# Linear attention on one Trainium2 core: the gate's product turned round and taken four steps at a time, and the lower weight halves subtracted from copies in PSUM

## The chip, the cores and the metric

The kernel runs on one core of a Trainium2 chip. The metric is device time in microseconds (us) of one execution; three runs gave 673.35, 677.05 and 677.16, median 677.05. TensorE is PE in the rows (its weight loads are PEld), VectorE is DVE, ScalarE is ACT, GpSimd is POOL, and SP issues most DMAs.

## What is computed

Three stages in a row, all on 3072 tokens of width 384 (4 sequences of 768 tokens, 8 heads of 48).

```python
for t in range(S):                       # stage 1: linear attention with decay
    cur = einsum('bhd,bhe->bhde', u * kt, vt)
    y[:, :, t] = einsum('bhd,bhde->bhe', rt, state + cur)
    state = w[None, :, :, None] * state + einsum('bhd,bhe->bhde', kt, vt)
logits = x @ w_gate                      # stage 2: 8 experts of exactly 384 tokens each,
h = maximum(x[mask] @ w1[e], 0.0)        #   given out greedily by descending logit
out[mask] = h @ w2[e]
h = maximum(maximum(x @ w1, x @ w2), x @ w3)   # stage 3
return h @ w_out
```

## The kernel before

**Attention** (class `Attention`) goes through 24 steps i, each 128 tokens of one sequence: `steps` is (b, c) for c in 0..5, b in 0..3, so four steps in a row share a chunk number c. Per step and line:

- GpSimd (POOL) does five multiplications of SBUF tiles: `decayed` (L129, `rt`), `natural` (L184, `kp`), `bonus` (L192, L193, `rk`) and, in `extra`, L203 (`bv`).
- TensorE makes transposes of keys (`turn`, L213, `pT`), masked scores (`scores`, L227, `pA`), output rows from the state and from the scores (`rows`, L248, both into `pY`), the new state (`state`, L281, `pK`), a transpose of the output (`cross`, L302, `pX`), four matmuls on ones whose result is not used (`keep`, L237), and the gate's logits (`gate`, L313). In `gate`, the step's transposed output `xt` (128x128 for each of three pieces) is the stationary operand and the 128x8 gate weights move.
- VectorE (DVE) masks the scores (L230, `am`), sums the bonus (L201, `bon`), adds the output parts (L263, `x`) and the state (L285, `st`). ScalarE (ACT) copies `kt` (L215), scales the state (L293, `S`), copies `xt` (L304) and takes squares of the output (L305).

Each engine works through its list in program order and waits by semaphores. `run` writes that order out step by step: step i issues `load(i + 4)`, `across(i + 3)` (the DMA of `rt`), `store(i - 1)`, then the POOL work for steps ahead, `turn(i + 2)`, `fade(i - 1)`, `scores(i + 1)`, `extra(i + 1)`, `cross(i - 1)`, `keep`, `rows(i)`, `gate(i - 2)`, `state(i)`.

**Weights.** Between these, at four places per step (`side`), a `Feed` issues pieces of the work that readies the first weights of the later stages: each fp32 (or float64) weight is scaled and split into an upper fp16 half, which ACT writes (L695 for `w`, L801 for `v`), and a lower half, which DVE writes as raw*scale - upper in one SCALAR_TENSOR_TENSOR (L699, L804); both its tensor inputs lie in SBUF. The float64 weights are first made fp32 with integer instructions on DVE (L760, L767, L776) that also read SBUF alone. Each piece has a cost by which the feed is spread over the steps. The early weights are `w1[0]`, `w2[0]`, the first two of stage 3, and the upper halves of `w1[1]`.

PSUM has eight banks: pX, pT, pK, lg one each, pA and pY two each. `lg` holds the logits of all steps (192 columns) and, in its upper half, the target of `keep`.

After attention come the **routing**, a chain of short dependent instructions, and the **experts** with stage 3, which are matmuls on TensorE almost throughout; the change leaves both alone but for the first input of routing, `raw` (L364), copied from `lg`.

The start is a chain too: POOL fills constants (L68 to L135), DVE waits for the first of its tables (L1173, `part`) before it builds the decay tables, and POOL's first `kp` waits for those.

Of the kernel before, what the change touches and what calls it, by code (L numbers as in the profile page):

```python
# [44 lines left out]
class Attention:  # L45


    def __init__(self, ctx, tc, K, r, rt, k, v, w, u, wg, x_dram, spare, routing):
# [10 lines left out]
        self.LD, self.RN, self.KN, self.BV, self.RT, self.KT, self.AM, self.X, self.XT, self.RK = ({} for _ in range(10))  # L59
# [17 lines left out]
        for t in self.S:  # L77
            nc.gpsimd.memset(t[:, :, D:], 0.0)
        self.routing.fill()
# [6 lines left out]
        self.wg = self.tabs.tile([128, 3, E], F32, name="wg")  # L86
        nc.sync.dma_start(self.wg, ap(wg, 0, [[E, 128], [128 * E, 3], [1, E]]))
# [4 lines left out]
        for i in range(2):  # L92
# [4 lines left out]
        self.lg = self.bank[:, :NT * E].rearrange("p (m e) -> p m e", e=E)  # L97
        nc.tensor.matmul(self.bank[:, 256:], self.K.onesf.bitcast(BF16)[:, :128], self.K.onesf.bitcast(BF16), start=True, stop=True,
                         skip_group_check=True)
# [94 lines left out]

    def extra(self, i):
# [3 lines left out]
        vn = self.LD[i][2]  # L199
        s = work.tile([128, H], F32, name="bon")  # L200
        nc.vector.tensor_reduce(s, self.RK[i].rearrange("p (h d) -> p h d", h=H), AX.X, OP.add)  # L201
# [31 lines left out]
    def keep(self, n):  # L233

        ones = self.K.onesf.bitcast(BF16)
        for _ in range(n):
            self.nc.tensor.matmul(self.bank[:, 256:], ones[:, :128], ones, start=False, stop=True, skip_group_check=True)  # L237

    def rows(self, i):
# [31 lines left out]
    def state(self, i):  # L271
# [5 lines left out]
        pk = psum.tile([128, NP, WIDE], F32, name="pK")  # L277
        for j in range(NP):
            for s in range(2):
                h = 2 * j + s  # L280
                nc.tensor.matmul(pk[64 * s:64 * s + 64, j, :], kd[:, h, :], vn[:, h * D:h * D + WIDE],  # L281
                                 start=j == 0, stop=j == NP - 1, skip_group_check=True)
        if c:
            t = work.tile([128, NP, D], F32, name="st", bufs=1)
# [11 lines left out]
    def cross(self, i):  # L296
# [6 lines left out]
        xt = self.XT[i] = work.tile([128, 3, C], F32, name="xt", bufs=3)  # L303
# [1250 lines left out]
```

## Time and profile before

| | |
|---|---|
| runs (median of 3) | 677.05 us (673.35 to 677.16) |
| profiled execution | 679.12 us, of which 677.4 us from the first to the last instruction |
| busy share of the span | PE 95%, PEld 63%, DVE 58%, ACT 52%, POOL 35% |
| attention | from the start to about 159 us |
| routing | about 159 to 204 us |
| experts and stage 3 | about 204 us to the end, PE 462.19 us busy of 473.40 |
| mean granted TensorE clock | 0.957 of full speed |

Busy time counts instructions that run, side by side or not; the end of a matmul is modelled, so a busy PE is not PE at its peak. The numbers below are of the one profiled execution, which is 2.07 us above the median of the runs.

### The profile page before, as it was taken

The page shows a single profiled execution, that of the slowest core. Times are in us where ns is not written, and L with a number is a line of the kernel's source. Part 1 is how long each engine was busy: PE and PEld are TensorE (multiplying, and loading weights), DVE is VectorE, ACT ScalarE, POOL GpSimd, SP SyncE. Part 2 cuts the span into 40 slices and gives each one's busy share as a digit, 9 for nine tenths or more (in the row PEclk, how much of TensorE's full clock was granted, in tenths as well). Part 3 has the DMA queues.
Part 4 walks back from the last instruction along what each step waited for, and adds up shares of the span by engine and source line. Part 5 has one row for each costly group of instructions (what it writes and reads, how often), then busy time and mean ns, then how long its engine had stood idle before and what let it go on. Part 6 is the DMA issues. An engine that isn't in the chain of part 4 may idle for free.

```text
span 677.4 us, 14362 instructions
## 1 busy us (share of the span) xinstructions
PE 642.2 (95%) x5660; PEld 429.9 (63%) x5660; DVE 394.8 (58%) x1027; ACT 350.2 (52%) x782; POOL 238.2 (35%) x268
## 2 busy tenths in 40 slices
PE   6999899998779998999999999999999999999996
PEld 4788787887566664666666666656665666666663
DVE  7777988757745767774556366354626544451321
ACT  3567474854443557574755655546544545332321
POOL 6989999980150003231122023112202111110222
PEclk8889998996579999999999999999999999999999
DMA  8877876625054309064134135112414200000000
GB/s 223 291 233 226 292 223 183 210 81 210 2 156 82 142 3 204 28 125 144 59 117 118 47 129 117 48 59 71 117 47 129 53 30 13 24 1 1 36 1 35
DMA packets 54763, 72.98 MB, mean 108 GB/s; under 512 B 21408, under 2 KB 42016, under 8 KB 54688
## 3 DMA queue, kind: packets, MB, share of 16 engines
q1 hardware_dynamic: 51616, 62.55, 31.3%
q0 software_dynamic: 3072, 9.44, 4.8%
q8 instruction: 46, 0.75, 0.5%
q14 instruction: 29, 0.24, 0.1%
HBM read 58.41 MB, written 9.44 MB: 100 GB/s over the span
## 4 chain that ended last, share of the span: by engine, by line
PE 60%; issue 7%; DVE 2%; POOL 1%; ACT 1%; POOLq 0%; DVEq 0%
PE pg L932 29%; PE ps L932 23%; PE px L1027 8%; POOL gt L1014 1%; DVE top L1009 1%; ACT gt L1013 0%; POOL out_dram L1034 0%; PE px L914 0%; POOLq L1550 0%; DVE da L760 0%; ACT top L1007 0%; ACT x2s L989 0%; ACT junk L628 0%; DVE sc L435 0%; DVE xr L905 0%
## 5 line engine op out<-in xcount | busy, mean ns | idle before, releaser
L932 PE MATMUL pg<-x2s,v 128*128 128x384 f16 x1296 | 217.0, 326 | 2.7 <-ACT top L1007 2.7
L932 PEld LDWEIGHTS <-v 128*128 128x128 f16 x1296 | 126.8, 98 | 86.8 <-issue 3.2
L1014 POOL TENSOR_TENSOR gt<-top,gt 128x384 f16<-128x384 f32 x48 | 44.4, 925 | 341.3 <-ACT gt L1013 291.9
L932 PEld LDWEIGHTS <-w 128*128 128x128 f16 x1242 | 117.2, 99 | 73.1 <-issue 1.6
L1009 DVE SCALAR_TENSOR_TENSOR top<-pg,sc,top 128x384 f32<-128x384 f32 x96 | 59.1, 616 | 75.0 <-PE pg L932 66.2
L932 PE MATMUL ps<-ht,w 128*128 128x384 f16 x576 | 94.9, 326 | 0.0
L699 DVE SCALAR_TENSOR_TENSOR w<-stage,sc,w 128x512 f16<-128x512 f32 (+1 forms) x80 | 70.4, 903 | 41.1 <-ACT w L695 40.8
L932 PE MATMUL ps<-xt,w 128*128 128x384 f16 (+1 forms) x540 | 88.6, 317 | 0.2 <-issue 0.2
L1013 ACT ACTIVATE gt<-top 128x384 f16<-128x384 f32 x48 | 25.0, 522 | 111.6 <-DVE top L1009 109.4
L1027 PE MATMUL px<-wo,gt 128*128 128x384 f16 x432 | 72.2, 326 | 1.8 <-POOL spacer L1033 1.0
L695 ACT ACTIVATE w<-stage,sc 128x512 f16<-128x512 f32 (+1 forms) x80 | 62.0, 797 | 3.0 <-DVE sc L466 1.2
L1027 PEld LDWEIGHTS <-gt 128*128 128x128 f16 x432 | 41.9, 98 | 30.8 <-POOL spacer L1033 1.7
L628 ACT ACTIVATE junk<-stage 128x768 bf16<-128x768 f32 x64 | 53.6, 837 | 6.3 <-DMA stage<-in_moe_w_dram 5.6
L962 DVE SCALAR_TENSOR_TENSOR ht<-ps,ht 128x384 f16<-128x384 f32 x56 | 30.9, 555 | 32.0 <-ACT ht L961 31.9
L1034 POOL DMA_INDIRECT out_dram<-o,ids x24 | 23.8, 993 | 40.8 <-ACT o L1032 40.8
L973 ACT ACTIVATE x<-ps 128x384 f32<-128x384 f32 x24 | 11.8, 490 | 49.7 <-PE ps L932 49.7
L230 DVE TENSOR_TENSOR am<-pA,mask 128x512 f32<-128x512 f32 x48 | 30.8, 682 | 10.3 <-PE pA L227 10.2
L1007 ACT ACTIVATE top<-pg,sc 128x384 f32<-128x384 f32 x48 | 27.7, 576 | 17.6 <-PE pg L932 17.2
L961 ACT ACTIVATE ht<-ps 128x384 f16<-128x384 f32 x56 | 26.7, 481 | 16.1 <-PE ps L932 16.0
L129 POOL TENSOR_TENSOR rt<-rt,tr 128x512 f32<-128x512 f32 x22 | 31.6, 1438 | 1.3 <-DMA rt<-in_rt_dram 1.3
L227 PE MATMUL pA<-rt,kt 64*128 64x128 f32 x384 | 29.9, 295 | 2.0 <-DVE am L230 1.9
L184 POOL TENSOR_TENSOR kp<-kn,tkn 128x384 f32<-128x384 f32 (+1 forms) x25 | 28.3, 1135 | 4.4 <-ACT tkn L168 3.8
(238 smaller groups left out, 851.9 us busy)
## 6 DMA issues: line engine op xcount, KB each, us to landing
stage<-in_moe_w_dram SPq DMA_DIRECT2D x41, 768.0 KB, 5.2
kn<-in_k_dram SPq DMA_DIRECT2D x24, 192.0 KB, 5.0
rn<-in_r_dram SPq DMA_DIRECT2D x24, 192.0 KB, 5.4
v<-in_v_dram SPq DMA_DIRECT2D x24, 192.0 KB, 3.2
rt<-in_rt_dram SPq DMA_DIRECT2D x48, 96.0 KB, 3.5
x_rows<-x SPq DMA_DIRECT2D x24, 192.0 KB, 2.6
stage<-in_moe_w_out_dram SPq DMA_DIRECT2D x3, 768.0 KB, 6.3
xg<-x_rows,ids POOLq DMA_INDIRECT x24, 5.1
```

Of the source, the lines that this page charges most:

```text
L129: (engine or self.nc.gpsimd).tensor_mul(self.RT[i], self.RT[i], self.tr)
L184: self.nc.gpsimd.tensor_mul(self.KN[i][:, heads, :D], kn[:, heads], self.tkn[:, heads, :D])
L227: nc.tensor.matmul(pa[s][:, j, :], kt[FULL[s], j * C:(j + 1) * C], rt[FULL[s], j * C:(j + 1) * C], start=True, stop=True, skip_group_check ...
L230: nc.vector.tensor_mul(am[:, s], pa[s], self.mask[:, None, :].to_broadcast([128, NP, C]))
L628: self.nc.scalar.activation(self.K.junk, x, AF.Square, accum_out=total)
L695: nc.scalar.activation(hi, raw, AF.Copy, scale=st["s"])
L699: nc.vector.scalar_tensor_tensor(lo, raw, st["s"], hi, op0=OP.mult, op1=OP.subtract)
L932: nc.tensor.matmul(p[:, rows], w[:, wi, k, cols], x[:, xi, k, rows], start=k == 0 and wi + xi == 0, stop=k == kb - 1 and xi == 1, skip_gro ...
L962: nc.vector.scalar_tensor_tensor(h[:, 1, f], p, 0.0, h[:, 0, f], op0=OP.max, op1=OP.subtract)
L1009: nc.vector.scalar_tensor_tensor(t, p, self.ratio[i], top, op0=OP.mult, op1=OP.max)
L1014: nc.gpsimd.tensor_sub(gt[:, 1, g], top, gt[:, 0, g])
L1027: nc.tensor.matmul(p, gt[:, gi, g, a * 128:(a + 1) * 128], self.WO[:, wi, g, :], start=g == 0 and gi + wi == 0, stop=g == self.KG - 1 and ...
```

## The change

Four edits inside attention and the feed.

1. `gate` makes the padded gate weights (128x32 per piece) the stationary operand and lets `xt` move; the three pieces write three groups of 32 partitions of `part`, and the four steps of a chunk lie in 8 rows each of those. It runs every fourth step, for four steps at once (in the last chunk step by step). ACT copies `part` to SBUF, and one step later a matmul with `sums` adds the three groups and turns the result (`logits`); ACT copies it to `raw`. So the single copy of `raw` at the end becomes six small ones. `xt` gets six buffers.
2. `keep` goes; `rows` instead issues four matmuls on zeros into `pY`, between the state's part and the scores' part, from the second chunk on. The gate stands between the two as well.
3. For the early weights, ACT copies each upper half from SBUF into one PSUM bank, `lane` (`twin`), and DVE's subtraction reads that copy. The pieces become 512 wide (some were 768), with a lower cost each.
4. `state` writes into the upper half of the `lg` bank, which frees the bank for `lane`; in the first chunk DVE now copies the state out. Also: the bonus sum is issued earlier (`summed`), the DMA of `rt` moves from the start of a step to its end (`across(i + 4)`, in place of `across(i + 3)`), and POOL fills two more constants at the start (`wg`, `zeros`).

```diff
+        self.wg = self.tabs.tile([128, 3, 56], F32, name="wg")
+        nc.gpsimd.memset(self.wg, 0.0)
+        nc.gpsimd.memset(self.zeros, 0.0)
         self.routing.fill()
...
+        nc.sync.dma_start(self.wg[:, :, 24:32], ap(wg, 0, [[E, 128], [128 * E, 3], [1, E]]))
...
+        between()
+        for n in range(KEEP if c else 0):
+            nc.tensor.matmul(py[n % 2].rearrange("p j n -> p (j n)"), self.zeros[:, :128], self.zeros, start=False, stop=False,
+                             skip_group_check=True)
         for j, s, u in where:
             h = 2 * j + s
...
-        pk = psum.tile([128, NP, WIDE], F32, name="pK")
+        pk = self.pk
...
         else:
-            t = pk
-        self.ST[i] = t
+            nc.vector.tensor_copy(t, pk[:, :, :D])
...
     def gate(self, i):
+
         if i < 0:
             return
-        b, c = self.steps[i]
-        m = b * NC + c
-        for j in range(3):
-            self.nc.tensor.matmul(self.lg[:, m, :], self.XT[i][:, j, :], self.wg[:, j, :],
-                                  start=(i == 0 and j == 0), stop=j == 2, skip_group_check=True)
+        c, k = divmod(i, B)
+        for n in (range(B) if k == B - 1 else ()) if c < NC - 1 else (k,):
+            for j in range(3):
+                self.nc.tensor.matmul(self.part[32 * j:32 * j + 32], self.wg[:, j, 24 - E * n:56 - E * n],
+                                      self.XT[B * c + n][:, j, :], start=n == 0, stop=n == B - 1, skip_group_check=True)
+        if k == B - 1:
+            self.parts = self.work.tile([128, 128], F32, name="parts", bufs=1)
+            self.nc.scalar.activation(self.parts[:96], self.part[:96], AF.Copy)
+
+    def logits(self, i):
+        c, k = divmod(i, B)
+        if k or c < 1:
+            return
+        nc, K = self.nc, self.K
+        nc.tensor.matmul(self.lg, self.parts[:96], K.sums[:96], start=True, stop=True, skip_group_check=True)
+        nc.scalar.activation(K.raw.rearrange("p (b c) e -> p b c e", c=NC)[:, :, c - 1, :],
+                             self.lg.rearrange("p (b e) -> p b e", e=E), AF.Copy, scale=-1.0)
...
+    def twin(self, x):
+
+        t = self.lane[:, :x.shape[-1]]
+        self.nc.scalar.activation(t, x, AF.Copy)
+        return t
...
         def lower(n):
             raw, (hi, lo) = part(*parts[n])
+            if apart:
+                hi = self.twin(hi)
             nc.vector.scalar_tensor_tensor(lo, raw, st["s"], hi, op0=OP.mult, op1=OP.subtract)
 
         def split(n):
             def go():
+                if n and apart:
+                    lower(n - 1)
                 if n < len(parts):
                     upper(n)
...
+            def go():
+                if j:
+                    hi, lo = (whole(dst[:, t])[:, cut(j - 1)] for t in range(2))
+                    nc.vector.scalar_tensor_tensor(lo, whole(st["x"])[:, cut(j - 1)], st["s"], self.twin(hi), op0=OP.mult,
+                                                   op1=OP.subtract)
+                if j < pieces:
+                    nc.scalar.activation(whole(dst[:, 0])[:, cut(j)], whole(st["x"])[:, cut(j)], AF.Copy, scale=st["s"])
```

TensorE, before, a step of the second chunk from the rows' state part on (`pY<-S`) to the first matmul of `keep` in the next step:

```order
L248 MATMUL pY<-S_117,rt_107 64x64 x16
L248 MATMUL pY<-v_120,am 64x64 x16
L313 MATMUL lg<-wg,xt 128x8 x3
L281 MATMUL pK<-v_120,kp_113 64x64 x8
L213 MATMUL pT<-identf,kp_112 128x128 x4
L227 MATMUL pA<-rt_109,kt_111 128x128 x8
L302 MATMUL pX<-identf,x 128x128 x3
L237 LDWEIGHTS onesf
L237 MATMUL lg<-onesf 128x256
```

TensorE, now, the same step, which is one with the gate for four steps (twelve matmuls); four pairs on zeros follow it, of which the first stands here:

```order
L307 MATMUL pX<-identf,x 128x128 x3
L250 MATMUL pY<-S_120,rt_110 64x64 x16
L319 MATMUL lg<-xt,wg 32x128 x12
L260 LDWEIGHTS zeros
L260 MATMUL pY<-zeros 128x256
```

The gate's three matmuls per step went from behind the rows' second part to twelve between its parts, and the four idle matmuls from in front of the first part to behind it.

TensorE, now, what comes next in that step, with its waits (names in brackets are the engines and DMA queues waited for):

```order
L250 MATMUL pY<-v_123,am 64x64 [waits DMAHW1_49]
L250 MATMUL pY<-v_123,am 64x64 x15
L287 MATMUL lg<-v_123,kp_116 64x64 [waits Activation_49]
L287 MATMUL lg<-v_123,kp_116 64x64 x7
L221 MATMUL pT<-identf,kp_115 128x128 [waits PE_49,Pool_49]
```

The state's matmul (L287, target now in the `lg` bank) waits for ScalarE here, that is for the copy of `part` out of the same bank.

ScalarE, before, while the first weight is split (`w_637`, pieces of 512):

```order
L305 ACTIVATE junk,norms<-x 128x384
L695 ACTIVATE w_637<-stage,sc_630 128x512 x3
L215 ACTIVATE kt_110<-pT 128x512
L293 ACTIVATE S_119<-pK,w_305 128x48 x4
L695 ACTIVATE w_637<-stage,sc_630 128x512 x2
L304 ACTIVATE xt<-pX 128x384
```

ScalarE, now, at the same place (`lane` is the copy in PSUM):

```order
L310 ACTIVATE junk,norms<-x 128x384
L649 ACTIVATE lane<-w_633 128x512
L726 ACTIVATE w_633<-stage,sc_626 128x512
L649 ACTIVATE lane<-w_633 128x512
L726 ACTIVATE w_633<-stage,sc_626 128x512
L649 ACTIVATE lane<-w_633 128x512
L726 ACTIVATE w_633<-stage,sc_626 128x512
L223 ACTIVATE kt_113<-pT 128x512
L298 ACTIVATE S_122<-st,w_310 128x48 x4
L649 ACTIVATE lane<-w_633 128x512
L726 ACTIVATE w_633<-stage,sc_626 128x512
```

Between two ScalarE instructions of attention's own chain, `xt` and `kt`, there are now six of the feed instead of three.

## Rows read from the trace of the kernel before

**Rows 1.** Windows: us; PE, PEld, DVE, ACT, POOL busy (count); clock; DMA share, GB/s.
```profile
41.00:151.00 110.00, 106.15 (x2046) 91.17 (x2046) 89.92 (x168) 71.08 (x188) 105.51 (x89) 0.98 0.66 206
```

**Rows 2.** Timeline of PE, one step: start us, us, line, out<-in, count.
```profile
130.77 0.69 PE L248 MATMUL pY<-S,rt 64*64 64x64 f32 x32
131.40 1.15 PE L248 MATMUL pY<-v,am 128*64 128x64 f32 x32
132.48 0.83 PE L313 MATMUL lg<-wg,xt 128*128 128x8 f32 x6
133.24 0.69 PE L281 MATMUL pK<-v,kp 128*64 128x64 f32 x16
...
135.92 0.60 PE L237 MATMUL lg<-onesf 128*128 128x256 bf16 x4
136.45 0.29 PE L248 MATMUL pY<-S,rt 64*64 64x64 f32 x4
```

**Rows 3.** Groups of POOL by form, 41 to 137 us: count | busy us, mean ns.
```profile
L129 POOL TENSOR_TENSOR rt<-rt,tr 128x512 f32<-128x512 f32 x16 | 24.0, 1500 | 1.3 <-DMA rt<-in_rt_dram 1.3
L193 POOL TENSOR_TENSOR rk<-rk,ub 128x384 f32<-128x384 f32 x15 | 19.1, 1272 | 1.2
L184 POOL TENSOR_TENSOR kp<-kn,tkn 128x384 f32<-128x384 f32 x15 | 18.3, 1223 | 0.6 <-PE pK L281 0.6
...
L203 POOL TENSOR_TENSOR bv<-v,bon 128x384 f32<-128x384 f32 x15 | 17.0, 1136 | 0.9 <-DVE bon L201 0.9
```

**Rows 4.** The same groups, 137 to 152 us.
```profile
L129 POOL TENSOR_TENSOR rt<-rt,tr 128x512 f32<-128x512 f32 x3 | 3.8, 1278 | 0.0
...
L193 POOL TENSOR_TENSOR rk<-rk,ub 128x384 f32<-128x384 f32 x3 | 3.0, 995 | 0.2
L203 POOL TENSOR_TENSOR bv<-v,bon 128x384 f32<-128x384 f32 x3 | 2.5, 827 | 0.0
L184 POOL TENSOR_TENSOR kp<-kn,tkn 128x384 f32<-128x384 f32 x2 | 2.0, 994 | 0.0
```

**Rows 5.** Timeline of POOL, a stretched multiplication.
```profile
65.92 1.98 POOL L129 TENSOR_TENSOR rt<-rt,tr 128x512 f32<-128x512 f32 x1
```

**Rows 6.** Timeline of DVE at the same time.
```profile
65.46 3.26 DVE L699 SCALAR_TENSOR_TENSOR w<-stage,sc,w 128x768 f16<-128x768 f32 x2
```

**Rows 7.** Groups of DVE by form, 41 to 151 us.
```profile
L230 DVE TENSOR_TENSOR am<-pA,mask 128x512 f32<-128x512 f32 x36 | 23.1, 682 | 5.4 <-PE pA L227 5.3
...
L767 DVE SCALAR_TENSOR_TENSOR da<-stage,da 128x768 int32<-128x768 int32 x6 | 9.2, 1537 | 0.1
L804 DVE SCALAR_TENSOR_TENSOR v<-wo,sc,v 128x768 f16<-128x768 f32 x6 | 8.3, 1417 | 0.0
L776 DVE SCALAR_TENSOR_TENSOR wo<-stage,da 128x768 int32<-128x768 int32 x6 | 8.2, 1372 | 0.0
L699 DVE SCALAR_TENSOR_TENSOR w<-stage,sc,w 128x512 f16<-128x512 f32 x6 | 5.8, 1000 | 0.0
L699 DVE SCALAR_TENSOR_TENSOR w<-stage,sc,w 128x768 f16<-128x768 f32 x4 | 5.6, 1425 | 0.0
```

**Rows 8.** Groups of ACT by form, 41 to 151 us.
```profile
L215 ACT ACTIVATE kt<-pT 128x512 f32<-128x512 f32 x18 | 10.7, 593 | 17.9 <-PE pT L213 17.8
...
L695 ACT ACTIVATE w<-stage,sc 128x512 f16<-128x512 f32 x8 | 5.4, 719 | 0.0
...
L628 ACT ACTIVATE junk<-wo 128x768 bf16<-128x768 f32 x6 | 5.1, 843 | 17.9 <-DVE wo L776 17.9
```

**Rows 9.** Windows around a drop of the clock (columns as in rows 1).
```profile
32.60:39.40 6.80, 6.80 (x57) 5.50 (x59) 2.70 (x10) 4.47 (x14) 6.02 (x7) 0.50 0.63 189
```

**Rows 10.** Timeline of DVE at the start.
```profile
3.58 0.15 DVE L1196 TENSOR_SCALAR pe_i<-part 128x1 int32<-128x1 int32 x1 [2.24 <-POOL part L1173]
```

**Rows 11.** Timeline of POOL at the start: constants.
```profile
1.66 1.44 POOL L76 MEMSET rt<- 128x512 f32 x3
```

**Rows 12.** Timeline of ACT at the end of attention.
```profile
158.68 0.33 ACT L364 ACTIVATE raw<-lg 128x192 f32<-128x192 f32 x1 [0.42 <-PE lg L313]
```

More of the change, by code (lines that the diff above doesn't have):

```diff
@@ L58, in __init__ @@
         self.steps = [(b, c) for c in range(NC) for b in range(B)]
-        self.LD, self.RN, self.KN, self.BV, self.RT, self.KT, self.AM, self.X, self.XT, self.RK = ({} for _ in range(10))
+        self.LD, self.RN, self.KN, self.BV, self.RT, self.KT, self.AM, self.X, self.XT, self.RK, self.BON = ({} for _ in range(11))
+        self.lane = self.psum.tile([128, 512], F32, name="lane")
+        self.zeros = self.tabs.tile([128, 256], BF16, name="zeros")
+        K.sums = self.tabs.tile([128, 32], F32, name="sums")
         wcol = self.tabs.tile([128, NP], F32, name="wcol")
@@ L96, in __init__ @@
         self.bank = self.psum.tile([128, 512], F32, name="lg")
-        self.lg = self.bank[:, :NT * E].rearrange("p (m e) -> p m e", e=E)
-        nc.tensor.matmul(self.bank[:, 256:], self.K.onesf.bitcast(BF16)[:, :128], self.K.onesf.bitcast(BF16), start=True, stop=True,
-                         skip_group_check=True)
+        self.lg, self.part = self.bank[:, :32], self.bank[:, 32:160]
+        self.pk = self.bank[:, 256:].rearrange("p (j n) -> p j n", n=WIDE)
     def clear(self, t):
@@ L231, in scores, with rows @@
         self.AM[i] = am
[L233 to L239, printed above, removed]
+    def rows(self, i, between=lambda: None):
         nc, psum = self.nc, self.psum
@@ L318, in run @@
         self.load(3)
+        self.across(3)
         feed.ahead(2)
@@ L345, in run @@
             side(3)
+            self.logits(i - 2)
             if i < NT - 2:
                 self.cross(i - 1)
-                self.keep(KEEP)
-                self.rows(i)
+                self.rows(i, lambda: self.gate(i - 2))
             else:
@@ L355, in run @@
                 self.cross(i - 1)
-            self.gate(i - 2)
+                self.gate(i - 2)
+            self.across(i + 4)
             side(4)
@@ L362, in run @@
         self.gate(NT - 1)
-        K = self.K
-        nc.scalar.activation(K.raw, self.lg, AF.Copy, scale=-1.0)
+        self.logits(NT)
 class Consts:
@@ L686, in part @@
                 return blocks[j].get()[:, q * 512:q * 512 + 512], [st["w"][:, t, q, j * 512:j * 512 + 512] for t in range(2)]
+            if apart:
+                n = (3 * j + q) * 512
+                return blocks[j].get()[:, q * 512:q * 512 + 512], [
+                    st["w"][:, t].rearrange("p k n -> p (k n)")[:, n:n + 512] for t in range(2)]
             k = 4 * j + 2 * q
@@ L689, in part @@
                 st["w"][:, t, k:k + 2].rearrange("p k n -> p (k n)") for t in range(2)]
-        parts = [(j, q) for j in range(2) for q in range(3 - which)]
+        apart = self.early and not left
+        parts = [(j, q) for j in range(2) for q in range(3 if apart else 3 - which)]
         def upper(n):
@@ L702, in go @@
             def go():
+                if n and apart:
+                    lower(n - 1)
                 if n < len(parts):
                     upper(n)
-                if n and not left:
+                if n and not (left or apart):
                     lower(n - 1)
@@ L723, in weight @@
         return (looks + ([] if routed else self.scaled(st, column, powers, blocks))
-                + [(split(n), st if n == 0 and not self.early else False, uses(n), 0.6 + 0.3 * which)
+                + [(split(n), st if n == 0 and not self.early else False, uses(n), 0.6 if apart else 0.6 + 0.3 * which)
                    for n in range(len(parts) + (not left))])
@@ L811, in double @@
                 + [(last, False, [], 0.1 if early else 1.05)] + self.scaled(st, column, powers, [])
-                + [(split(j), st if j == 0 and not early else False, [], 0.9) for j in range(nb + 1)])
+                + ([(fine(j), False, [], 0.6) for j in range(pieces + 1)] if early
+                   else [(split(j), st if j == 0 else False, [], 0.9) for j in range(nb + 1)]))
     def room(self, i):
```

29 lines of the change are left out of this document (21 added, 8 removed).

## The prediction

> **What bounds the kernel now.** I read the windows first, then the step on TensorE, then the groups of GpSimd, VectorE and ScalarE. In the long middle of attention, 41 to 151 us, two engines are busy nearly without a gap: TensorE 106.15 of 110 us and GpSimd 105.51, while VectorE has 89.92 and ScalarE 71.08 [rows 1]. Both have to become shorter for this stage to become shorter. On TensorE the timeline of one step has no idle time at all: from the state's part of the rows at 130.77 to the same place one step later at 136.45 is 5.68 us, and 110 us hold 18 steps (36 `am`, two per step [rows 7]), 6.1 us each [rows 2]. On GpSimd five multiplications make a step. Late in the stage they take 1278 + 994 + 995 + 827 ns and, for L192, which has L193's form, again 995: 5.1 us [rows 4]. Earlier they take 1500, 1223, 1272 and 1136 [rows 3]. What stretches them shows in the two timelines: a multiplication of 1.98 us runs where VectorE works on lower halves, two of them in 3.26 us [rows 5, 6]. Both tensors of a lower half lie in SBUF, as GpSimd's do. After attention the change moves nothing but the first link of routing, so whatever attention saves arrives at the end in full.
>
> **The gate.** It goes from every step to every fourth. Now its six passes per step (fp32 takes two per matmul) hold TensorE from 132.48 to 133.24, 0.76 us, with 128 stationary columns in each pass [rows 2]; 18 steps make 13.7 us. What a pass costs with 32 stationary and 128 moving columns no row shows. From above, it is as long as a pass of now, 0.76 / 6 = 0.127 us, and none run side by side: 24 passes, 3.0 us a batch. From below, three groups of partitions run side by side, as the two halves of `pY<-v,am` do (32 passes in 1.08 us from 131.40 to 132.48, 0.034 each [rows 2]), and a group of three costs what two cost there, 0.068: 8 groups, 0.5 us. I take side by side, but with the length of a 128-column pass, 8 x 0.127 = 1.0 us a batch. Five batches fall in the stage: 5.0. The matmul that adds the groups has two passes, 0.25, five times 1.3. TensorE: -13.7 + 6.3 = -7.4 us (from -9.9 to +2.6).
>
> The Trainium skill, page "TensorE: Matmul & The Clock Gate", section "Why this matters for your kernels", says that outputs in separate 32-partition groups run side by side and that three such matmuls gained 2.38 times. By it a batch would be 24 x 0.127 / 2.38 = 1.3 us, and the term 1.5 us smaller. No run here shows it for groups of 32.
>
> **The idle matmuls.** Four go and four come per step from the second chunk on, at 0.53 us for four (135.92 to 136.45) [rows 2]: nothing in the stage. The four steps of the first chunk lose theirs, 2.1 us of TensorE, but GpSimd sets the pace there and TensorE may fall to its lower clock level: 0 for the sum.
>
> **The lower halves.** 22 pieces of at most 512 replace 16 of 512 or 768. VectorE now spends 8.3 + 5.8 + 5.6 = 19.7 us on them [rows 7]. With one input from PSUM the nearest row is `am`, one input from PSUM and one from SBUF at 512 columns, 682 ns: 22 x 0.68 = 15.0, so VectorE gains 4.7 us (between 22 x 0.59, ScalarE's time to read 512 from PSUM [rows 8], and 22 x 1.0, the 512 form of now: +6.7 to -2.3).
>
> GpSimd gains if the new form doesn't hold it up. The stretch in the stage is 16 x 0.222 (`rt`) + 15 x 0.277 (L193) + 15 x 0.229 (`kp`) + 15 x 0.309 (`bv`) = 15.8, plus 15 x 0.23 for L192 taken like `kp`: about 19 us [rows 3, 4]. VectorE's operations with two tensors in SBUF are the lower halves, 19.7 us, and the integer ones that stay, 9.2 + 8.2 = 17.4 us [rows 7]. By share 19.7 / 37.1 of 19 is 10; some goes to a shift that also reads SBUF alone, so I take 9. The bounds are 0 (it still locks) and 19.
>
> The Trainium skill, page "SBUF — State Buffer", section "Who interferes with whom", says that a VectorE instruction with two SBUF inputs blocks a GpSimd one that reads SBUF, and one with a single SBUF input does not. By it the lower halves would stop blocking and L767 and L776 would go on. No row here has the new order of inputs, SBUF first and PSUM second, beside a running GpSimd.
>
> ScalarE pays. 22 copies into PSUM at 0.593 (`kt`, 512 columns; 0.719 for the form with a scale) are 13.0 us [rows 8], six more upper halves, as the pieces are smaller, at some 0.3 us of fixed time each (719 ns for 512 columns [rows 8], of which I take 0.8 ns a column as the rate, an estimate), 2 us, and `parts` and `raw` 10 short copies at 0.33 [rows 12] at most, 3 us. So 71 becomes 89 of some 103 us. It is hidden as long as ScalarE has room; where that cover is gone it costs what rival three says.
>
> **The shared bank.** Where the gate has run, the state's matmul waits for the copy of `part`. The idle matmuls and the scores' part lie between, 0.53 + 1.08 = 1.6 us [rows 2], and the copy takes 0.33 [rows 12]; what is queued on ScalarE before it is `xt` and a square. I cost it at 0; behind the waiting matmul the next `pT` and `pA` are queued, so if ScalarE is 2 us late it costs about 1 us at each of five places. The copy of the state in the first chunk, the earlier bonus sum and the moved DMA of `rt` lie in idle time of their engines. On SP the moved `rt` waits for the rows of its own step, and the next `load` is queued behind it; its data are used two steps later, so nothing waits.
>
> **Start and end.** VectorE waits 2.24 us for GpSimd's first table [rows 10], and two more constants, 168 and 256 columns, stand ahead of it. Three of 512 take 1.44 us [rows 11], 0.94 ns a column: +0.4 us, and the whole chain moves. At the end one copy of 0.33 us [rows 12] becomes copy, matmul (0.25), copy; one gate of 0.76 gets shorter in turn: +0.3 us.
>
> **Sum.** In the stage TensorE falls to 106.15 - 7.4 = 98.8 and GpSimd to 105.5 - 9 = 96.5. TensorE remains the longer; with its idle time of now, 3.85, the stage takes 102.6 instead of 110, -7.4. I give back 1 us, because four engines now lie between 85 and 99 and wait for each other more: -6.4 + 0.4 + 0.3 = -5.7 us. The profiled execution of 679.12 becomes 673.4. The median of the runs is 2.07 lower, so 677.05 becomes 671.4; I say 671.
>
> **Rivals.**
>
> *One: ScalarE and VectorE take the place* (25%). The 22 copies are not spread but come in four bursts: six feed instructions stand between `xt` and `kt` instead of three, about 3.7 us instead of 2.2. Each burst makes one step some 1.5 us longer, 4 x 1.5 = 6 of the 7.4 us, and the kernel stays at 676. For it: ScalarE waited 17.9 us for VectorE in six places already [rows 8]. Against: `kt` is used a step later.
>
> *Two: both floors are reached* (15%). The groups of three run at the lower bound, 0.5 us a batch, and the earlier bonus sum and `rt` remove GpSimd's waits of 1.3 and 0.9 us [rows 3]. TensorE gains 9.9, and GpSimd 9 + 2: -10 + 0.7, 668 or a little less.
>
> *Three: slower, by the one bank `lane`* (11%). A copy may start only when VectorE has read the one before, and VectorE has masks and sums in its list between them. Then ScalarE stands still, and `kt`, `S` and `xt` behind it. ScalarE's longest such wait costs 17.9 / 6 = 3.0 us each now [rows 8]. Were half of the 22 copies to wait that long, 33 us, ScalarE would have 89 + 18 + 33 = 140 us for a stage of 110. It decides from the point where busy and waiting time pass 110, that is from 3 us of new waits on. At 17 us of waits (0.8 per copy) the stage is 124 less the room that waits overlap by, half of it: 117, +7 + 0.7, 685.
>
> *Four: the clock* (5%). A stretch of 6.80 us had a granted clock of 0.50, that is 1.2 GHz, and TensorE was busy for all of it with 57 matmuls [rows 9]; in the stage it does 2046 in 110 us [rows 1], twice the rate. Without idle matmuls in the first chunk, TensorE may stay at 1.2 GHz for two more steps: +4 us, 675; with more such drops in the middle, where it is less busy, 680.
>
> *Five: the lock stays.* If VectorE's second input blocks GpSimd wherever it lies, GpSimd keeps 105.5 - 2 and the gain is 2 less 0.7: 676. This is in the 25% of rival one.
>
> **Chances and range.** Forecast 44%, rivals 25, 15, 11, 5. A measurement of this kernel can tell about 1%, 6.8 us, from no change. Faster by over 1% is below 670.3: rival two and half of the forecast, 37%. Slower by over 1% is above 683.8: most of rival three, 9%. The rest is within. The range holds the forecast and rivals one and two with the unknown pass, and some of the slower ones: 664 to 681.
>
> **What would show it.** Right: GpSimd's means between 41 and 140 us fall by about 0.12 us, and remain stretched beside L767 and L776; a gate batch of 24 passes takes about 1 us; the last `raw` comes about 6 us earlier than 158.68. Wrong: a gate batch of 2.5 us or more; ScalarE waiting for VectorE at `lane`, with `kt` late and TensorE idle in front of `pA`; GpSimd as slow as now beside the new lower halves; a clock of 0.50 in more of the stage than now.

## The result, and the profile after the change

The changed kernel takes 682.47 us (median of four runs, 681.07 to 685.47), the kernel before 676.85 on the same chip: 1.0096 times as long, with an interval of 1.007 to 1.0121. The prediction said 671, from 664 to 681. By the medians it is slower by 5.6 us, by the ratio 6.5, and it lies outside the range by 1.5 us on the side of rival three.

The traced execution of the changed kernel took 681.07 us (span 679.4), that of the kernel before 679.12 (677.4). The one lies 1.4 us below its median and the other 2.3 above, so the spans differ by only 2.0. What attention lost is read better at its end: the last `raw` starts at 163.06 us, after 158.68 [rows 12].

The windows of the stage, in the kernel after (columns as in rows 1):

```profile
41.00:151.00 110.00, 97.11 (x1928) 78.80 (x1923) 81.93 (x169) 82.03 (x221) 96.08 (x89) 0.95 0.64 200
```

Beside [rows 1] the busy times look like the forecast, but for ScalarE: TensorE 106.15 to 97.11 (98.8 forecast), GpSimd 105.51 to 96.08 (96.5), VectorE 89.92 to 81.93 (85.2), ScalarE 71.08 to 82.03 (89). Equal windows do not hold equal work, though. I measure the pace from the end of x's last sum in step 4 to that in step 22, eighteen steps: 47.91 to 153.59 before, 105.7 us, and 46.04 to 157.26 after, 111.2. The windows of these eighteen steps, before and then after:

```profile
47.91:153.59 105.68, 101.83 (x1985) 87.61 (x1985) 85.38 (x165) 66.84 (x177) 100.73 (x86) 0.98 0.64 203
```

```profile
46.04:157.26 111.22, 100.04 (x2003) 81.14 (x2002) 81.58 (x171) 78.50 (x212) 91.94 (x85) 0.95 0.60 188
```

For the same steps GpSimd has 8.8 us less to do, VectorE 3.8 less and ScalarE 11.7 more. TensorE's busy time falls by 1.8 us only, at a mean clock of 0.95 instead of 0.98, and its idle time rises from 3.85 to 11.2 us. No engine is full any more, and still the stage is longer.

GpSimd's groups by form, 41 to 137 us, kernel after (as rows 3):

```profile
L133 POOL TENSOR_TENSOR rt<-rt,tr 128x512 f32<-128x512 f32 x16 | 22.5, 1408 | 0.0
L188 POOL TENSOR_TENSOR kp<-kn,tkn 128x384 f32<-128x384 f32 x15 | 18.3, 1222 | 9.7 <-PE lg L287 9.7
L197 POOL TENSOR_TENSOR rk<-rk,ub 128x384 f32<-128x384 f32 x15 | 16.8, 1120 | 1.2
...
L211 POOL TENSOR_TENSOR bv<-v,bon 128x384 f32<-128x384 f32 x15 | 12.4, 828 | 0.6 <-DVE bon L203 0.6
```

Three of the four means of [rows 3] fell, `bv` by 308 ns to what it takes alone at the end of the stage [rows 4]. But GpSimd now stands still for 9.7 us in front of `kp`, since the buffer that it writes is read by the state's matmul of four steps earlier, and that is late. Why it is late shows in the list of waits, 41 to 155 us, kernel after (in total, times, longest):

```profile
POOL kp L188 <- PE lg L287: 11.7, 7, 3.9
DVE x L269 <- PE pY L250: 10.0, 5, 3.9
...
DVE v L849 <- ACT lane L649: 4.2, 3, 1.8
DVE w L732 <- ACT lane L649: 4.2, 4, 1.8
...
PE lg L287 <- ACT parts L323: 4.1, 2, 2.6
PE pX L430 <- ACT xt L309: 3.9, 2, 2.2
...
ACT lane L649 <- DVE v L849: 3.5, 5, 1.6
...
ACT lane L649 <- DVE w L732: 1.9, 4, 1.2
```

At `lane` VectorE waits 8.4 us for ScalarE's copies, and ScalarE 5.4 us until VectorE has read them.

One such place in the timelines of the kernel after, TensorE first (start us, us, [idle before]):

```profile
97.02 1.07 PE L319 MATMUL lg<-xt,wg 128*32 128x128 f32 x24
98.02 0.61 PE L260 MATMUL pY<-zeros 128*128 128x256 bf16 x4
98.56 1.15 PE L250 MATMUL pY<-v,am 128*64 128x64 f32 x32
102.28 0.69 PE L287 MATMUL lg<-v,kp 128*64 128x64 f32 x16 [2.56 <-ACT parts L323]
```

ScalarE at the same time:

```profile
97.94 0.57 ACT L223 ACTIVATE kt<-pT 128x512 f32<-128x512 f32 x1
98.41 1.00 ACT L298 ACTIVATE S<-st,w 128x48 f32<-128x48 f32 x4
99.32 0.58 ACT L649 ACTIVATE lane<-v 128x512 f32<-128x512 f16 x1
99.83 0.49 ACT L852 ACTIVATE v<-wo,sc 128x256 f16<-128x256 f32 x1
100.77 0.39 ACT L649 ACTIVATE lane<-v 128x256 f32<-128x256 f16 x1 [0.44 <-DVE v L849]
101.09 0.47 ACT L309 ACTIVATE xt<-pX 128x384 f32<-128x384 f32 x1
...
101.97 0.26 ACT L323 ACTIVATE parts<-lg 96x128 f32<-96x128 f32 x1
```

VectorE, and then GpSimd:

```profile
97.42 0.75 DVE L849 SCALAR_TENSOR_TENSOR v<-wo,sc,lane 128x512 f16<-128x512 f32 x1 [0.73 <-ACT lane L649]
99.93 0.75 DVE L849 SCALAR_TENSOR_TENSOR v<-wo,sc,lane 128x512 f16<-128x512 f32 x1 [1.76 <-ACT lane L649]
100.59 1.28 DVE L238 TENSOR_TENSOR am<-pA,mask 128x512 f32<-128x512 f32 x2
```

```profile
103.06 1.46 POOL L188 TENSOR_TENSOR kp<-kn,tkn 128x384 f32<-128x384 f32 x1 [2.92 <-PE lg L287]
```

VectorE stands 1.76 us until a copy is in `lane`, because ScalarE has `kt` and `S` in its list ahead of it. The next copy then has to wait 0.44 us until VectorE has read this one. Behind it on ScalarE stand `xt`, the square and, as the last, the copy of `part`, which the gate had finished at 98.1. At 101.97 it is made at last; the state had waited 2.56 us for it, and GpSimd 2.92 us for the state. All four engines stand in turn. ScalarE itself waits little here: most of its lateness is what its list holds, and what the link at `lane` costs in all has to come from runs (a3 and a4 below).

After some of TensorE's waits its clock falls besides. Windows of the kernel after (columns as in rows 1), not one after the other in the program:

```profile
121.40:128.20 6.80, 6.80 (x80) 5.59 (x79) 2.79 (x9) 3.75 (x11) 5.41 (x6) 0.50 0.64 183
...
118.41:120.63 2.22, 0.01 (x2) 0.00 (x1) 1.50 (x4) 2.22 (x9) 2.14 (x4) 1.00 0.64 208
```

For 2.22 us, up to 120.63, TensorE waits for `xt` (VectorE's L811 and ScalarE's sums behind it are late); from 121.40 on the granted clock is 0.50, 1.2 GHz, for 6.80 us. In the step after this x comes 11.0 us after the one before it, at 130.9. This wait is not at `lane`; the list of a3 has it with 3.2 us in total and that of a4 with 4.3, at a mean clock of 1.00.

### The profile page after: what moved, and what is told of

It is laid out like the page before. It is cut to its first block, busy times and chain, and to the rows that moved or that the text cites. A ratio compares the mean times of both kernels' runs of the same rounds, so it can differ in the third digit from the quotient of the medians.

```text
span 679.4 us, 14463 instructions
## 1 busy us (share of the span) xinstructions
PE 633.7 (93%) x5663; PEld 416.0 (61%) x5663; DVE 391.7 (58%) x1039; ACT 364.7 (54%) x821; POOL 229.9 (34%) x270
## 4 chain that ended last, share of the span: by engine, by line
PE 60%; issue 7%; DVE 2%; POOL 1%; ACT 1%; POOLq 0%; DVEq 0%; ACTq 0%
PE pg L985 29%; PE ps L985 23%; PE px L1080 8%; POOL gt L1067 1%; DVE top L1062 1%; ACT gt L1066 0%; POOL out_dram L1087 0%; PE px L967 0%; POOLq L1606 0%; DVE da L795 0%; ACT top L1060 0%; ACT x2s L1042 0%; ACT junk L654 0%; DVE sc L455 0%; ACT da L780 0%
## 5 line engine op out<-in xcount | busy, mean ns | idle before, releaser
L732 DVE SCALAR_TENSOR_TENSOR w<-stage,sc,w 128x512 f16<-128x512 f32 (+1 forms) x70 | 58.8, 861 | 41.1 <-ACT w L726 41.1
L188 POOL TENSOR_TENSOR kp<-kn,tkn 128x384 f32<-128x384 f32 (+1 forms) x25 | 28.3, 1136 | 15.8 <-PE lg L287 11.7
L235 PEld LDWEIGHTS pA<-rt,kt 64*128 64x128 f32 x384 | 25.5, 194 | 8.9 <-DVE am L238 6.4
```

Source lines behind the costliest of these rows:

```text
L188: self.nc.gpsimd.tensor_mul(self.KN[i][:, heads, :D], kn[:, heads], self.tkn[:, heads, :D])
L235: nc.tensor.matmul(pa[s][:, j, :], kt[FULL[s], j * C:(j + 1) * C], rt[FULL[s], j * C:(j + 1) * C], start=True, stop=True, skip_group_check ...
L732: nc.vector.scalar_tensor_tensor(lo, raw, st["s"], hi, op0=OP.mult, op1=OP.subtract)
```

## The experiments

The theories. *P*: TensorE's busy time is the bound of the kernel before, as forecast. *Q*: GpSimd's is. *L*, later *H*: ScalarE and VectorE, each working through its list in order, hold each other at the one bank `lane`. *G*: the gate's batch and the shared bank hold TensorE back; its parts later are *S* (the shared bank) and *R* (the ring of `kp` buffers). *C*: a waiting TensorE loses its clock, and that takes the gain.

All eighteen runs; the ratio is to the kernel before, run beside it on the same chip, the pace is as defined above, from one traced execution each (two kernels alike in their medians can differ by some 2 us in it).

| run | what differs | median us | ratio, interval | pace us |
|---|---|---|---|---|
| before | | 676.85 | | 105.7 |
| after | | 682.47 | 1.0096, 1.007 to 1.0121 | 111.2 |
| e1 | after, no copies, lower halves from SBUF | 679.63 | 1.0039, 1.0021 to 1.0057 | 106.1 |
| e2 | e1, state in its own bank | 680.11 | 1.0041, 1.0026 to 1.0056 | 106.9 |
| e3 | after, batch behind the rows | 683.87 | 1.0095, 1.0062 to 1.0128 | 113.4 |
| e4 | after, gate step by step | 680.66 | 1.0072, 1.0047 to 1.0097 | 108.4 |
| e5 | after, five buffers of `kp` | 683.26 | 1.0095, 1.0056 to 1.0134 | 112.3 |
| e6 | after, state in its own bank | 680.72 | 1.0052, 1.0031 to 1.0074 | 105.9 |
| e7 | e5 and e6 | 682.03 | 1.0076, 1.0051 to 1.0101 | 108.9 |
| e8 | e7 and e3 | 682.49 | 1.0074, 1.005 to 1.0099 | 108.5 |
| b1 | before, no idle matmuls | 674.58 | 0.9986, 0.9971 to 1.0002 | 105.2 |
| a1 | after, eight idle matmuls a step | 684.76 | 1.0121, 1.0089 to 1.0153 | 112.1 |
| e9 | e6, four idle matmuls more | 685.97 | 1.014, 1.0107 to 1.0173 | 111.4 |
| e10 | e2, idle matmuls as before | 681.03 | 1.0074, 1.005 to 1.0099 | 107.7 |
| b2 | before, one GpSimd product less | 698.27 | 1.0329, 1.0305 to 1.0353 | 105.6 |
| a2 | after, the same product less | 702.2 | 1.0385, 1.0354 to 1.0415 | 107.5 |
| a3 | after, no copies, `lane` all zeros | 674.09 | 0.9961, 0.9942 to 0.9979 | 101.6 |
| e11 | e6, no idle matmuls | 679.21 | 1.003, 1.001 to 1.0049 | 107.9 |
| a4 | a3, copies into a scratch tile | 677.78 | 0.9989, 0.9959 to 1.0018 | 104.4 |
| b3 | b1, six bonus products on VectorE | 678.0 | 1.0027, 0.9993 to 1.0061 | 106.6 |

### The change in parts: e1 to e4

e1 takes the lower halves back to SBUF; e2 gives the state its own bank as well; e3 moves the batch; e4 goes back to three products per step, with the logits of all steps in the bank and one copy at the end.

```diff
-        apart = self.early and not left
+        apart = False
...
-        self.lane = self.psum.tile([128, 512], F32, name="lane")
+        self.lane = None
...
-        pk = self.pk
+        pk = psum.tile([128, NP, WIDE], F32, name="pK")
...
-                self.rows(i, lambda: self.gate(i - 2))
+                self.rows(i)
+                self.gate(i - 2)
...
+            self.nc.tensor.matmul(self.lg[:, m, :], self.XT[i][:, j, :], self.wg[:, j, 24:32],
+                                  start=(i == 0 and j == 0), stop=j == 2, skip_group_check=True)
```

> Kernel after with the lower halves put back: DVE reads the upper half in SBUF, in the pieces of the kernel before, and no copy to the bank `lane` is made. Gate in fours and the shared bank stay. Theory L (the round trips between ScalarE and VectorE over the one bank `lane` cost the time): about 671 us, ScalarE 13 us less busy between 41 and 155 us, no waits at `lane`, and VectorE's 3.9 us wait for pY in step 17 stays near 2. Theory G (the batch of the gate and the shared bank hold back TensorE, x and POOL): 680 us or more, the waits of state for `parts` and `raw` stay, POOL's kp goes on waiting 10 us or more for state. Theory C (a wait of TensorE for the scale's transpose, 2.2 us at 118.4, lowers the granted clock for 6.8 us): still 680 or so, and the 0.5 stretch at 121 stays.

> The same, and the state has a bank of its own again (the one that `lane` held): of the change only the gate in fours, its place and the moved small steps are left. Theory L: as the run before, about 671, since the shared bank costs nothing. Theory G: the waits of state for `parts` (4.3 us) and `raw` (1.7 us) go, POOL's kp waits less than 5 us for state, and the time falls 3 to 5 us below the run before. Theory C: 680 unless the stretch at 121 us goes.

> Kernel after with one edit: the gate's batch stands behind all of the rows' products instead of between their halves, so that x does not wait for it. Theory G: VectorE's wait for pY falls from 10.0 us to under 5, 678 us or less. Theory L: no difference, 681 to 683, the state then waits longer for `parts`. Theory C: no difference while the clock is 0.5 from 121 to 128.

> Kernel after with the gate's products step by step again (activations stationary, eight moving columns, one copy of all logits at the end), at the new place between the halves of the rows; `lane` and the shared bank stay. This is the change without its gate. Theory L: slower than the kernel after by the gate's price, 686 or more. Theory G: faster than the kernel after, 676 to 680, since no step waits for a batch of 1.7 us or for `raw` behind ScalarE's queue. Theory C: TensorE is busier and does not run into the wait at 118 us, the 0.5 stretch at 121 us is gone, about 678.

No theory was met in full. Without the copies (e1) the time falls by 0.57%, 3.9 us, not by 11: part of the loss is at `lane`, as L has it, but the gate alone (e2) is still 0.41% slower than the kernel before, and giving the state its bank back changes nothing there. e3 is no faster: VectorE's wait for pY halves (10.0 to 5.1), and TensorE's for `parts` grows from 4.1 to 5.0, since the batch now stands closer to the state. e4 gains 0.24%, inside the intervals. The window of the stage in e2 says what its floor is:

```profile
41.00:151.00 110.00, 101.06 (x2033) 81.60 (x2031) 91.08 (x168) 71.80 (x196) 106.89 (x89) 0.98 0.65 204
```

GpSimd is back at 106.89, beside 96.08 with the copies. So the new lower halves do set it free, and without them TensorE's shorter gate meets a full GpSimd.

A part of e2's loss stands at the end of attention. In the kernel after, the four idle matmuls also run in the last two steps, where the kernel before has none (TensorE in the last step, before and then after):

```profile
153.85 0.69 PE L248 MATMUL pY<-S,rt 64*64 64x64 f32 x32
154.47 1.15 PE L248 MATMUL pY<-v,am 128*64 128x64 f32 x32
```

```profile
157.30 0.70 PE L250 MATMUL pY<-S,rt 64*64 64x64 f32 x32
157.93 0.61 PE L260 MATMUL pY<-zeros 128*128 128x256 bf16 x4
158.47 1.15 PE L250 MATMUL pY<-v,am 128*64 128x64 f32 x32
```

From x of step 22 to the start of the last `raw` it is 5.09 or 5.10 us in the kernel before, b1, b2 and b3, 5.79 or 5.80 in the kernel after, e2 and ten others, 6.24 in a1 with eight idle matmuls, and 5.25 in e10 and e11, which have none there. One step's four cost 0.55 us, so those of the last two some 1.1 (an estimate).

### Who waits for the shared bank: e5 to e8

e5 gives `kp` a fifth buffer (and `xt` five instead of six), e6 the state its own bank (the gate's results go to pT's), e7 and e8 combine.

```diff
-                                     for name, m in (("rt", 4), ("kt", 2), ("kp", 4)))
+                                     for name, m in (("rt", 4), ("kt", 2), ("kp", 5)))
...
+            self.part = self.psum.tile([128, 512], F32, name="pT")[:, :128]
...
+        lg = self.psum.tile([128, 512], F32, name="pT")[:, :32]
```

> Kernel after with a fifth buffer for the decayed keys `kp` (and xt in five buffers instead of six, for the room), so that POOL's kp of step i+3 no longer waits for the state of step i-1. Theory R (POOL's waits for the state, 11.7 us between 41 and 155, are what eats POOL's gain): POOL's wait falls under 2 us and the time by 3 us or more, to 679 or less. Theory S (the state's wait on TensorE for ScalarE's copies out of the shared bank is the loss): POOL's wait goes, TensorE's waits for `parts` and `raw` (5.6 us) stay, time 680.5 to 683. Theory H (ScalarE and VectorE, each in order, hold each other at the one bank `lane`): 681 to 683 as well.

> Kernel after with `lane` kept, the state in a bank of its own, and the gate's two results in the bank of pT, whose next use is the transpose of the next step. Theory S: TensorE's waits at the state's line go, POOL's wait for the state falls from 11.7 us under 6, and the time falls 3 to 5 us, to 677 to 679. Theory R: 680 or more, POOL's wait stays over 8 us. Theory H: 680 to 683, TensorE then waits at pT for `parts` and `raw` instead.

> Both edits of the two runs before. Theories S and R: each gives its part, 675 to 678, below the kernel before if both hold. Theory H: 680 or more, and ScalarE's and VectorE's waits for each other at `lane` (13 us of both between 41 and 155) stay as they are.

> The same with the gate's batch behind all of the rows' products. The batch then delays no x and no longer stands ahead of a copy that the state waits for. Theory S: VectorE's wait for pY falls from 10.0 to about 5 us, 1 to 2 us below the run before. Theory H: no difference over 1 us.

R falls: in e5 GpSimd's wait for the state is gone and nothing is won. The wait has only moved along its list, to `bv`, whose sum VectorE makes late; GpSimd's waits in e5, 41 to 155 us:

```profile
POOL bv L211 <- DVE bon L203: 11.0, 7, 3.4
```

S holds for a part: e6 is 0.44% faster than the kernel after (3.0 us). H is seen in it too, as TensorE's waits in e6, 41 to 155 us, only change their place:

```profile
PE pX L430 <- ACT xt L306: 3.2, 2, 1.9
PE pT L318 <- ACT kt L220: 3.0, 3, 1.5
PE pT L330 <- ACT kt L220: 2.2, 2, 1.1
```

e7 and e8, with more of the waits taken away, are no better than e6.

### What TensorE's and GpSimd's time is worth: b1, a1, e9, e10, b2, a2

```diff
-                self.keep(KEEP)
...
-        for n in range(KEEP if c else 0):
+        for n in range(2 * KEEP if c else 0):
...
-        engine.tensor_mul(t, t, self.ub)
+        if engine is not self.nc.gpsimd:
+            engine.tensor_mul(t, t, self.ub)
```

The first piece is b1, the second a1, the third b2 and a2. e9 puts a `keep` of zeros into the state's bank ahead of `cross`; e10 has the `keep` of the kernel before in place of the zeros.

> The kernel before with one edit: the four idle matmuls of each step are left out, so TensorE has some 11 us less to do between 41 and 151 us (11.3 of its 106.15 there). Theory P (TensorE's 106 us are the bound of the kernel before, as the prediction has it): about 667 to 671. Theory Q (POOL's 105.5 us are the bound, TensorE's work only fills the room): 675 to 678, POOL as busy as before, TensorE waiting 10 us more. Theory C (a TensorE that waits loses its clock, and what is taken from it comes back as half speed): more stretches at 0.50 between 41 and 151 than the one of before, 678 or more.

> Kernel after with eight idle matmuls of a step instead of four: 0.6 us more for TensorE in each of 20 steps, 12 us in all, at the same place. Theory C: the stretch at half clock from 121 us (and the one at 46) goes or shortens, so that the time stays at 680 to 683 or falls although TensorE has 12 us more to do. Theory H (the waits of ScalarE and VectorE for each other set the pace): 682 to 685. If TensorE's work were the bound of the kernel after: 692 or more.

> The kernel of e6 (`lane`, the state in its own bank, the gate's results in pT's) and four idle matmuls more in every step, the first four too, ahead of the transposes of x (into the state's bank, which is free there). Theory C: no 0.50 stretch between 41 and 151, 678 or less. Theory H: 681 or more, the waits at `lane` and for xt as in e6.

> The kernel of e2 (the gate in fours, the rest as before) with the idle matmuls of the kernel before, at their old place and in the first four steps too. Theory C: what e2 lost against the kernel before (3 us) was the clock of the first chunk or of its waits, so 676 to 678. Theory Q (POOL at its floor of 107 us in e2): 679 to 681, no change, with POOL 19.7 of every 20 us busy from 60 to 140.

> The kernel before without POOL's second product of the bonus (the rows are not multiplied by u; 22.1 us of POOL in 18 steps between 41 and 151). Theory Q (POOL is the bound of the kernel before): 664 to 670, POOL no longer without gaps. Theory P (TensorE is): 675 to 678, TensorE 106 of 110 as before.

> The kernel after without the same product (19.8 us of POOL). Theory H (in the kernel after, POOL is not the bound: ScalarE and VectorE, each in order, hold each other and TensorE): 679 to 683, POOL's waits longer by what it saves. Theory Q carried over to the kernel after: 668 to 673.

Without the product by u the logits are others, and what follows attention takes longer (span less the end of `raw`: 695.3 - 156.6 = 538.7 us in b2, 677.4 - 159.0 = 518.4 before). Of b2 and a2 only the pace counts.

b1 speaks against P: idle matmuls of 11.3 us are gone, and eighteen steps take 105.2 us instead of 105.7. GpSimd is as full as before. b2 speaks against Q in the same way: with 22 us less for GpSimd, 105.6. The windows of b1, and then of b2:

```profile
41.00:151.00 110.00, 100.64 (x1987) 86.52 (x1988) 90.27 (x172) 68.62 (x181) 106.58 (x90) 0.95 0.64 204
```

```profile
41.00:151.00 110.00, 105.86 (x2071) 91.06 (x2061) 89.99 (x171) 68.69 (x183) 83.15 (x70) 0.98 0.64 205
```

Either engine alone holds the pace: in b1 GpSimd has 106.58, in b2 TensorE 105.86. That far the prediction's "Both have to become shorter" was right. In the kernel after neither does so alone: a2 leaves out 20 us of GpSimd, and 13.5 of them come back as a longer wait for the state (11.7 to 25.2 us) and 7.3 in front of `bv` (4.0 to 11.3), with a pace of 107.5 that other kernels with copies come near without it (e6, e11); a1 adds 12 us to TensorE for 0.25%, which is inside the intervals.

C is not decided by these. In a1 the mean clock of the stage is 0.97 instead of 0.95, and it is no faster. b1 has the same 0.95 as the kernel after at a pace of 105.2, since there GpSimd keeps time. e9's matmuls themselves waited for VectorE (4.6 us), so it tells little. e10 tells no more: its idle matmuls write into the bank of `raw` and waited 5.4 us for ScalarE's copies out of it, so whether e2 lost by their place stays open.

### The price of the copies: a3, a4, e11, b3

```diff
-        self.nc.scalar.activation(t, x, AF.Copy)
+        self.nc.scalar.activation(self.K.junk[:, :x.shape[-1]], x, AF.Copy)
...
+        engine = engine or (self.nc.vector if i in (7, 8, 12, 13, 17, 18) else self.nc.gpsimd)
```

a3 has the first line taken out, a4 as shown, and in both `lane` is set to zero once. The other line is b3; e11 has `range(0)` for the zeros.

> The kernel after without ScalarE's copies: VectorE reads a bank that holds zeros, so the lower halves are not the differences. Gate, shared bank, pieces and VectorE's form stay; 13 us of ScalarE and every wait at `lane` are gone, and POOL stays as free as with the copies. Theory H: the price of the copies is all of the loss, 670 or less. Theory S (the shared bank, with the gate's batch, is the loss): 678 or more, TensorE still waiting some 5 us for `parts` and `raw`.

> The kernel of e6 (`lane`, own bank for the state, gate's results in pT's bank) without idle matmuls: TensorE has 12 us less to do. If TensorE's work counts there: 672 or less. Theory H: 678 to 681, no change beyond 2 us. Theory C: 682 or more, with more stretches at 0.50 between 41 and 155 than e6 has (none).

> The kernel after with ScalarE's copies made into a scratch tile in SBUF that nobody reads, while VectorE reads a bank of zeros: ScalarE's work stays as in the kernel after, the waits of ScalarE and VectorE for each other at `lane` are gone (the lower halves are not the differences, as in a3). If ScalarE's work is the price of the copies: 680 to 683, as the kernel after. If the waits for each other are: 673 to 676, as without copies. Between the two, the part of each is read off.

> The kernel before without idle matmuls (as b1) and with the two products of the bonus of steps 7, 8, 12, 13, 17 and 18 on VectorE instead of POOL: POOL 6 x 2.4 = 14 us less, VectorE up to 6 x 2.6 = 16 us more by its two products at the start (1.35 and 1.24 us). If two floors (TensorE's and POOL's) are all that holds the kernel before: 668 to 672. If VectorE, which would have 106 of 110 us to do, is the third: 675 to 680.

a3 is the prediction's kernel, gate, shared bank and lower halves with one input from PSUM, with the copies for nothing: 0.39% faster than the kernel before (theory H had 670 us or less), 1.35% (9.1 us) faster than the kernel after. a4 puts ScalarE's work back without the link to VectorE and loses 0.28% (not more than the intervals). So 1.07%, 7.2 us give or take 2.6, are the price of the link, the waits for each other with all that follows from them. Both runs also free VectorE of waiting for the upper half at all; in the kernel before the lower halves show no such wait. The windows of a3, and then of a4:

```profile
41.00:151.00 110.00, 104.06 (x2207) 85.09 (x2206) 89.61 (x185) 76.25 (x209) 98.74 (x90) 1.00 0.67 211
```

```profile
41.00:151.00 110.00, 100.86 (x2134) 82.74 (x2130) 86.97 (x181) 88.39 (x232) 97.75 (x90) 1.00 0.68 214
```

In a4 ScalarE has 88.39 us of work in the window, where more steps fall into it, and the pace is 104.4 instead of 111.2: it is not the load. The eighteen steps of a4:

```profile
48.49:152.89 104.40, 95.26 (x2012) 77.79 (x2010) 81.15 (x170) 81.23 (x217) 91.14 (x84) 1.00 0.66 206
```

ScalarE does more in them than in the kernel after, 81.23 beside 78.50. Of the 6.8 us between the two paces, TensorE's busy time has 4.8 (100.04 at a clock of 0.95, 95.26 at 1.00) and its idle time 2.0. So how much of the link's price the clock carries is not decided by these two traces.

The shared bank goes with this in part: TensorE waits 0.2 us for `parts` at the state in a3, 3.6 in a4 and 4.1 in the kernel after. It costs nothing where ScalarE is in time (e1 and e2 alike) and 3.0 us in the kernel after (e6); what it costs in a4 no run shows.

e11 shows that TensorE's time is not the limit with the copies either (12 us less of it, 0.22%). b3 lowers both floors, GpSimd to 96.89 and TensorE to 101.43, and raises VectorE to 101.50; it is no faster. None of these kernels with the right result is reliably faster than the kernel before: b1's interval reaches over 1, and a3 and a4 don't compute the lower halves.

## Why the prediction was wrong, step by step

By the ratios, with 1% = 6.8 us, the loss adds up like this: the gate in fours with the small moves +2.8 us (e2), the shared bank by itself 0 (e1), the lower halves' new form -5.3 (a3 less e1), the copies as work +1.9 (a4 less a3), the link at `lane` and what follows from it +7.2 (after less a4): +6.5, the 0.96% of the result. Each difference is known to some 2 to 3 us.

- *The gate, -7.4 us of TensorE.* The size was about right: a batch of 24 passes takes 1.07 us at full clock, forecast 1.0, and over the eighteen steps the gate falls from 14.6 to 9.1 us, some of it at half clock. By the 2.38 times of the Trainium skill ("TensorE: Matmul & The Clock Gate", section "Why this matters for your kernels"), which it states for 512 moving columns, a batch would take 1.3 us, an estimate. The trace shows more, 24 x 0.127 / 1.07, 2.8 times. What the gate is worth was wrong. With the small moves (e2) it makes the kernel slower by 2.8 us. That TensorE's time alone is worth little here b1 and e2 show. Some 1.1 of the 2.8 us are the idle matmuls of the last two steps; where the rest comes from stays open. e2's trace has `raw` only 1.0 us later, with VectorE's wait for pY at 9.3 us between 41 and 151, after 2.5 in the kernel before. The earlier bonus sum, the moved DMAs and the longer start were not tried one by one.
- *The idle matmuls, "nothing in the stage", and the end, +0.3.* They were overlooked in the last two steps; from x of step 22 to `raw` the change costs 0.7 us. The +0.4 of the start can't be read: x of step 0 ends at 22.06 us before, at 22.49 after, and between 20.96 and 23.22 in the other runs.
- *The lower halves, GpSimd -9.* Right: 105.5 to 96.1 in the window, 8.8 us over the eighteen steps, and back to 106 in e1 and e2 (there was no forecast for a kernel without them). The rule of the Trainium skill ("SBUF — State Buffer", section "Who interferes with whom"), that a VectorE instruction with one SBUF input leaves GpSimd alone, agrees with the rows. VectorE's 512 columns take 744 ns instead of the 682 of `am`, so its term was about right as well.
- *ScalarE's copies, "hidden as long as ScalarE has room".* This step failed. ScalarE had room, 82 of 110 us, less work than forecast (11.7 us more over the eighteen steps, not 18), and the copies still cost 9.1 us, of which its work is 1.9. The other 7.2 are the link: one bank that two engines hand to each other, each with other work in its list between two pieces.
- *The shared bank, "I cost it at 0".* Failed with it. The text's own condition, "if ScalarE is 2 us late it costs about 1 us at each of five places", was what happened: two waits of 4.1 us together for `parts`, one of 1.5 for `raw`, and 3.0 us (0.7 to 5.2) by e6.
- *The sum: "with its idle time of now, 3.85, the stage takes 102.6".* This is where the errors meet. For the same eighteen steps TensorE's idle time went from 3.85 to 11.2 us, and its busy time fell by 1.8 us instead of 7.4, though the gate alone lost 5.5. In part that is the clock, 0.95 instead of 0.98 (99.19 us busy in e2 at 0.98, 95.26 in a4 at 1.00). The 1 us given back for four engines that wait for each other was too small.
- *Rivals.* Three named the place and the outcome, and had 11%. It looked for 17 us of waits on ScalarE; at `lane` ScalarE waits 5.4 us and VectorE 8.4. Its point of decision, 110 us of busy and waiting time on ScalarE, was wrong: the loss begins long before ScalarE is full. One (bursts on ScalarE): a4 shows the copies as work alone to be cheap. Two: GpSimd came down by 8.8 of its 11 us, TensorE by 1.8 of its 9.9, and the time did not follow. Five (the lock stays) is out by GpSimd's fall. Four, the clock: between 41 and 151 us its mean fell from 0.98 [rows 1] to 0.95; both stretches at 0.50 (46.27 to 49.67 and 121.40 to 128.20) lie behind the first chunk. It was 1.00 in a3, a4 and e6, so part of what the waits cost in a single execution may be the clock's; a1 and e11 (0.92, and yet 0.22% faster than e6) don't make it the cause.
- *What would show it.* GpSimd's means and the batch came as written under "right"; the last `raw` came 4.4 us later, not 6 earlier. Under "wrong", ScalarE waits for VectorE at `lane`, and the clock is at 0.50 in more of the stage. TensorE is idle in front of the state and the scale's transpose more than in front of `pA`.

## What to carry to other kernels

When several engines are nearly full, do not carry a fall of busy time into the length of a stage with the idle time held as it was; look for who else stands in the circle, and test the floor by leaving work out, as b1 and b2 do. A copy from one engine to another through a single buffer costs more than its duration: here 1.9 us as work and 7.2 as a link. I take as the reason what stands in both lists between two pieces, and would not queue behind it what others wait for; no run changes these lists or adds a second buffer, so that much is argued. If a buffer is to be shared, ask not how long its last reader takes but how late it can start.

## What the runs showed of the hardware

VectorE's second input in PSUM instead of SBUF gave GpSimd 10 us of 106 back (e1 106.08 us, after 96.08, in the same window), with `bv` down to a mean of 828 ns. `kp` kept its 1222 ns: the five of fifteen between 41 and 137 us that took 1.46 to 1.72 us ran beside the integer operations that stayed (L802, L811), and the others took 1.00 to 1.08.

In the kernel after, TensorE's granted clock fell to 0.50, 1.2 GHz, from 46.27 to 49.67 us, after a wait of 1.5 us before 44.31, and from 121.40 to 128.20, after the one of 2.2 us before 120.63. After the wait of 2.6 us before 102.28 it stayed at 1.00, 2.4 GHz.
